# A linear-attention and top-1 expert kernel: weights held by rank of load, three first layers in a row at the change to the experts, and late weight loads from slot 3 on

## The chip, the core and the metric

The kernel runs on one core of a Trainium2 chip, as one program in one launch. What counts is the device time of that launch in microseconds, from inputs in the chip's memory (HBM) to outputs in it. The kernel before takes 1004.49 us (median of three runs, 1004.49 to 1005.99). Its profiled execution spans 1002.1 us.

A core has five engines with instruction streams of their own, which wait for each other by semaphores: TensorE (PE; its weight loads are listed apart as PEld), VectorE (DVE), ScalarE (ACT), GpSimd (POOL) and SyncE (SP). Sixteen DMA engines move data; in this kernel SP and POOL issue the transfers.

## What is computed

Eight batches of eight heads with 576 rows of 64 features go through attention without softmax. The result, 4608 rows of 512, goes through eight experts, and each row through one of them:

```python
def phi(x, c, s):
    r = np.maximum(x, 0.0)
    return np.concatenate([r * c, r * s], axis=-1)   # c, s: cos, sin of the position
kv  = np.einsum('bhsf,bhsd->bhfd', phi(k), v);  z = np.sum(phi(k), axis=2)
x   = einsum(phi(q), kv) / (einsum(phi(q), z) + 1e-6)       # 4608 x 512
logits = x @ w_gate;  e_idx = argmax(logits)                # the expert of a row
gate_w = softmax(logits)[e_idx];  eom = sigmoid(x @ w_output_gate)
for e in range(8):                                          # F = 1024
    h = np.maximum(x[mask] @ w1[e], 0.0);  ye = h @ w2[e]
    out[mask] = gate_w[mask, None] * eom[mask, e, None] * ye
```

The inputs are drawn once and are the same in every run. With them the experts get 305, 493, 580, 0, 986, 569, 398 and 1277 rows, which fill 39 tiles of 128 rows if each expert begins a tile of its own. q, k, v and the weights are fp32; 28.3 MB of q, k and v are read, and 33.6 MB of weights, which become 16.8 MB of fp16 on the way in.

## The kernel before

**Weights.** At the very start GpSimd issues 16 transfers (L121, L122) that bring all weights into two resident tiles, `w1t` and `w2t`, and turn fp32 to fp16 as they do.

**Attention (L136 to L253).** For each batch there are five chunks of 128 rows, the last of 64. SyncE loads `qt`, `kt` and `vt` of a chunk (double buffered, runs of 256 bytes). ScalarE makes `qp` and VectorE `kp`: relu, times cosine into 64 columns and times sine into 64 more. TensorE multiplies `kp` with `vt` for each head (L171), and VectorE adds the product into `kvzg` (L173). TensorE turns `qp` of each head (L178), and ScalarE and VectorE in turn copy the result to `qpt` (L181, L183). When all five chunks of a batch are in, each head's `kvzg` is turned (L187), copied (L189) and multiplied with the gate weights (L191), so that the gates' logits come out of the same product as the rows. Then for each chunk `fx` = `qpt` x `kvzg` (L204); VectorE divides, sums the logits of eight heads (L215), finds the expert and the coefficient, and writes `xch` (L250), which goes to `x_dram`. All of it is fp32, apart from `xch`.

**Routing (L255 to L358).** After the last chunk the counts of the experts are summed over all 40 chunks and every chunk gets the positions of its rows. GpSimd scatters each chunk's row numbers and coefficients to the table `bucket` in HBM (L348). `dst_i`, `pack` and `ni` have one buffer each, so a chunk's scatter must have landed before the next chunk's positions may be written. The table is then read back to `bidx`.

**Experts (L366 to L416).** 42 slots of 128 rows, the largest number that could be needed. A slot's rows are gathered from `x_dram` (L371), turned (L377) and copied (L390), multiplied with 512 x 1024 weights (L395), put through relu (L399), turned (L384), copied (L387), multiplied with 1024 x 512 weights (L406), scaled (L410) and scattered to the output (L411). All is fp16 with fp32 sums. The two layers of neighbouring slots alternate on TensorE.

The order of work on the engines is left to a scheduler that follows the program order and the tiles' dependencies.

Of the kernel before, what the change touches and what calls it, by code (L numbers as in the profile page):

```python
# [10 lines left out]
F32 = mybir.dt.float32  # L12
F16 = mybir.dt.float16
I32 = mybir.dt.int32
ALU = mybir.AluOpType
AF = mybir.ActivationFunctionType
AX = mybir.AxisListType
# [3 lines left out]
def kernel(  # L21
# [21 lines left out]
    E = 8  # L43
    F = 1024
    P = 128
    NCH = 5
    ROWS = [128, 128, 128, 128, 64]
    NG = B * NCH
    NSLOT = 42
    CAP = NSLOT * P  # L50

    constp = ctx.enter_context(tc.tile_pool(name="constp", bufs=1))
    wpool = ctx.enter_context(tc.tile_pool(name="wpool", bufs=1))
    tabs = ctx.enter_context(tc.tile_pool(name="tabs", bufs=1))
    dram = ctx.enter_context(tc.tile_pool(name="drampool", bufs=1, space=bass.MemoryType.DRAM))

    x_dram = dram.tile([N, DM], F16, name="x_dram")
    bucket = dram.tile([CAP, 2], F32, name="bucket")

    ident = constp.tile([P, P], F32, name="ident")  # L60
    make_identity(nc, ident[:])
    ident16 = constp.tile([P, P], F16, name="ident16")
    make_identity(nc, ident16[:])
    u128 = constp.tile([P, P], F32, name="u128")
    make_upper_triangular(nc, u128[:], val=1.0, diag=False)
    ones128 = constp.tile([P, P], F32, name="ones128")
    GP.memset(ones128[:], 1.0)

    s_i = constp.tile([P, NCH], I32, name="s_i")
    GP.iota(s_i[:], pattern=[[128, NCH]], base=0, channel_multiplier=1)  # L70
    th = constp.tile([P, NCH], F32, name="th")
# [3 lines left out]
    th2 = constp.tile([P, NCH], F32, name="th2")  # L75
# [5 lines left out]
    cosc = constp.tile([P, NCH], F32, name="cosc")  # L81
    sinc = constp.tile([P, NCH], F32, name="sinc")

    def поly(dst, coeffs, extra_mul, nm):
        acc = constp.tile([P, NCH], F32, name=nm)
        DVE.memset(acc[:], 0.0)
        for cc in reversed(coeffs):
            DVE.tensor_mul(acc[:], acc[:], th2[:])
            DVE.tensor_scalar_add(acc[:], acc[:], float(cc))
        DVE.tensor_mul(acc[:], acc[:], th2[:])  # L90
        DVE.tensor_scalar_add(acc[:], acc[:], 1.0)
        if extra_mul is not None:
            DVE.tensor_mul(dst[:], acc[:], extra_mul[:])
        else:
            DVE.tensor_copy(dst[:], acc[:])

    поly(sinc, sin_c, th, "acc_s")
    поly(cosc, cos_c, None, "acc_c")

    wg2 = constp.tile([P, H, 16], F32, name="wg2")  # L100
    SP.dma_start(wg2[0:64, :, 0:8], moe_w_gate.rearrange("(h p) e -> p h e", p=64))
    SP.dma_start(wg2[0:64, :, 8:16],
                 moe_w_output_gate.rearrange("(h p) e -> p h e", p=64))

    iota8 = constp.tile([P, E], F32, name="iota8")
    _i8 = constp.tile([P, E], I32, name="_i8")
    GP.iota(_i8[:], pattern=[[1, E]], base=0, channel_multiplier=0)
    DVE.tensor_copy(iota8[:], _i8[:])
    iota_slot = constp.tile([P, 1], F32, name="iota_slot")
    _is = constp.tile([P, 1], I32, name="_is")  # L110
    GP.iota(_is[:], pattern=[[1, 1]], base=0, channel_multiplier=128)
    DVE.tensor_copy(iota_slot[:], _is[:])
    mvals = constp.tile([P, NSLOT], F32, name="mvals")
    _im = constp.tile([P, NSLOT], I32, name="_im")
    GP.iota(_im[:], pattern=[[128, NSLOT]], base=0, channel_multiplier=0)
    DVE.tensor_copy(mvals[:], _im[:])

    w1t = wpool.tile([P, 4, E, F], F16, name="w1t")
    w2t = wpool.tile([P, 8, E, DM], F16, name="w2t")
    for e in range(E):  # L120
        GP.dma_start(w1t[:, :, e, :], moe_w1[e].rearrange("(c p) f -> p c f", p=128))  # L121
        GP.dma_start(w2t[:, :, e, :], moe_w2[e].rearrange("(c p) d2 -> p c d2", p=128))  # L122

    coef_tab = tabs.tile([P, NG], F32, name="coef_tab")
    oh_tab = tabs.tile([P, NG, E], F32, name="oh_tab")
    bidx = tabs.tile([P, NSLOT, 2], F32, name="bidx")
    gidx_i = tabs.tile([P, NSLOT], I32, name="gidx_i")
    sidx_i = tabs.tile([P, NSLOT], I32, name="sidx_i")
    slote_i = tabs.tile([P, 1], I32, name="slote_i")

    with tc.tile_pool(name="attn_b", bufs=2) as ap, \
         tc.tile_pool(name="attn_c", bufs=2) as ap2, \
         tc.tile_pool(name="pskv", bufs=3, space=bass.MemoryType.PSUM) as pskv, \
         tc.tile_pool(name="psgen", bufs=5, space=bass.MemoryType.PSUM) as psgen:

        for b in range(B):  # L136
            qpt = ap.tile([P, H, 576], F32, name=f"qpt{b}", tag="qpt")
            kvzg = ap.tile([P, H, 81], F32, name=f"kvzg{b}", tag="kvzg", bufs=1)
            GP.memset(kvzg[:], 0.0)

            for c in range(NCH):
                rows = ROWS[c]
                s0 = c * 128
                qt = ap2.tile([P, H, D], F32, name=f"qt{b}_{c}", tag="qt")
                kt = ap2.tile([P, H, D], F32, name=f"kt{b}_{c}", tag="kt")
                vt = ap2.tile([P, H, 65], F32, name=f"vt{b}_{c}", tag="vt")
# [300 lines left out]
```

## Time and profile before

| | us | from |
|---|---|---|
| time, median of three | 1004.49 | times |
| span | 1002.1 | profile |
| PE busy | 662.7 (66%), 3257 instructions | profile |
| VectorE busy | 377.0 (38%), 2049 instructions | profile |
| ScalarE busy | 177.9 (18%) | profile |
| GpSimd busy | 152.0 (15%) | profile |
| HBM read, written | 67.45 MB, 15.81 MB | profile |

A share of the span is an average over stages that have different limits. Two parts of the profile help against this. One cuts the span in 40 slices and gives each engine's busy share as a digit. The other, the chain of waits, goes back from the last instruction, at each step to what released it, and so tells which work or which transfer the end waited for at any time. A third table gives the busy time of each engine between two times that the reader picks. The profile's groups of instructions give the mean duration of one. Matmuls are pipelined, so the mean duration of one is longer than the time from one to the next. The pace of a run of them is read from the chain.

### The profile page before, as it was taken

The page shows a single profiled execution, that of the slowest core. Times are in us where ns is not written, and L with a number is a line of the kernel's source. Part 1 is how long each engine was busy: PE and PEld are TensorE (multiplying, and loading weights), DVE is VectorE, ACT ScalarE, POOL GpSimd, SP SyncE. Part 2 cuts the span into 40 slices and gives each one's busy share as a digit, 9 for nine tenths or more (in the row PEclk, how much of TensorE's full clock was granted, in tenths as well). Part 3 has the DMA queues.
Part 4 walks back from the last instruction along what each step waited for, and adds up shares of the span by engine and source line. Part 5 has one row for each costly group of instructions (what it writes and reads, how often), then busy time and mean ns, then how long its engine had stood idle before and what let it go on. Part 6 is the DMA issues. An engine that isn't in the chain of part 4 may idle for free.

```text
span 1002.1 us, 11193 instructions
## 1 busy us (share of the span) xinstructions
PE 662.7 (66%) x3257; PEld 496.6 (50%) x3257; DVE 377.0 (38%) x2049; ACT 177.9 (18%) x509; POOL 152.0 (15%) x245
## 2 busy tenths in 40 slices
PE   0113187997979979799797884223221099999994
PEld 0013176785867858578575683222211045555552
DVE  3101028456283562835528364111111033443342
ACT  1111001314123141231412210000000022222221
POOL 4110000000000000000000001222222134444441
PEclk9999999999999999999999999999999999999998
DMA  9999931412414124141241000000000112222220
GB/s 173 200 200 200 78 79 34 101 42 61 85 50 95 43 61 85 51 95 43 61 84 51 11 17 9 0 0 2 0 0 1 6 63 91 84 83 88 86 85 21
DMA packets 148858, 65.64 MB, mean 65 GB/s; under 512 B 128254, under 2 KB 141054, under 8 KB 148800
## 3 DMA queue, kind: packets, MB, share of 16 engines
q1 hardware_dynamic: 129600, 33.16, 17.5%
q0 software_dynamic: 19200, 31.77, 13.8%
q8 instruction: 29, 0.48, 0.2%
q14 instruction: 29, 0.24, 0.1%
HBM read 67.45 MB, written 15.81 MB: 83 GB/s over the span
## 4 chain that ended last, share of the span: by engine, by line
PE 50%; DMA 26%; DVE 13%; ACT 5%; issue 4%; SPq 1%; POOLq 0%; POOL 0%; ACTq 0%; DVEq 0%
DMA bucket<-pack,dst_i 14%; PE kvp L171 13%; PE fx L204 9%; PE hp L395 7%; DMA qt<-in_q_dram 7%; PE yp L406 7%; PE tp L178 5%; PE kvgp L191 4%; DVE xch L250 4%; DVE glog L215 2%; PE tpk L187 2%; DMA kt<-in_k_dram 2%; PE htsp L384 2%; DMA vt<-in_v_dram 2%; ACT kvt L189 1%
## 5 line engine op out<-in xcount | busy, mean ns | idle before, releaser
L178 PE MATMUL tp<-ident,qp 128*128 128x128 f32 (+1 forms) x320 | 101.2, 423 | 113.9 <-ACT qpt L181 36.9
L171 PE MATMUL kvp<-vt,kp 128*128 128x65 f32 (+1 forms) x640 | 145.6, 412 | 30.5 <-DMA vt<-in_v_dram 28.1
L171 PEld LDWEIGHTS kvp<-vt,kp 128*128 128x128 f32 (+1 forms) x640 | 143.3, 332 | 32.9 <-issue 32.0
L204 PE MATMUL fx<-kvzg,qpt 128*128 128x81 f32 (+1 forms) x640 | 136.1, 406 | 7.4 <-DVE glog L215 7.4
L204 PEld LDWEIGHTS fx<-kvzg,qpt 128*128 128x128 f32 (+1 forms) x640 | 128.9, 310 | 12.2 <-PE fx L204 10.6
L178 PEld LDWEIGHTS tp<-ident,qp 128*128 128x128 f32 (+1 forms) x320 | 55.4, 206 | 158.2 <-ACT qpt L181 74.1
L399 ACT ACTIVATE hs<-hp 128x512 f16<-128x512 f32 x84 | 50.2, 597 | 331.5 <-PE hp L395 331.5
L250 DVE TENSOR_SCALAR xch<-fx,rc 128x64 f16<-128x64 f32 (+1 forms) x320 | 86.8, 273 | 0.0
L395 PE MATMUL hp<-w1t,xts 128*128 x336 | 81.2, 385 | 7.5 <-DVE xts L390 7.5
L406 PE MATMUL yp<-w2t,hts 128*128 x336 | 79.4, 379 | 1.1 <-DVE hts L387 1.1
L173 DVE TENSOR_TENSOR kvzg<-kvzg,kvp 128x260 f32<-128x260 f32 x80 | 32.9, 418 | 110.5 <-PE kvp L171 110.5
L410 DVE TENSOR_SCALAR ysb<-yp,bidx 128x512 f32<-128x512 f32 x42 | 31.5, 751 | 112.8 <-PE yp L406 112.8
L215 DVE SCALAR_TENSOR_TENSOR glog<-fx,rc,glog 128x16 f32<-128x16 f32 (+1 forms) x280 | 62.9, 225 | 0.3
L181 ACT COPY qpt<-tp 128x128 f32<-128x128 f32 (+1 forms) x160 | 39.8, 252 | 119.5 <-PE tp L178 119.5
L183 DVE COPY qpt<-tp 128x128 f32<-128x128 f32 (+1 forms) x160 | 38.6, 266 | 47.8 <-PE tp L178 45.3
L341 DVE CAST dst_i<-dst_f 128x1 int32<-128x1 f32 (+1 forms) x40 | 6.1, 152 | 131.8 <-DMA bucket<-pack,dst_i 131.8
L406 PEld LDWEIGHTS <-hts 128*128 128x128 f16 x336 | 32.8, 98 | 40.6 <-DVE hts L387 1.2
L153 POOL MEMSET vt<- 128x8 f32 x40 | 4.4, 113 | 314.2 <-PE kvp L171 263.2
L395 PEld LDWEIGHTS <-xts 128*128 128x128 f16 x336 | 32.1, 98 | 39.7 <-DVE xts L390 9.1
L411 POOL DMA_INDIRECT out_dram<-ysb,sidx_i x42 | 42.6, 1014 | 56.1 <-DVE ysb L410 37.2
L348 POOL DMA_INDIRECT bucket<-pack,dst_i x40 | 38.6, 966 | 79.3 <-DVE dst_f L338 55.6
L371 POOL DMA_INDIRECT xg<-x_dram,gidx_i x42 | 40.8, 972 | 62.6 <-PE xtsp L377 45.9
(234 smaller groups left out, 661.1 us busy)
## 6 DMA issues: line engine op xcount, KB each, us to landing
qt<-in_q_dram SPq DMA_DIRECT2D x32, 256.0 KB, 3.9
w1t<-in_moe_w_dram POOLq DMA_DIRECT2D x8, 1024.0 KB, 46.4
kt<-in_k_dram SPq DMA_DIRECT2D x32, 256.0 KB, 3.5
vt<-in_v_dram SPq DMA_DIRECT2D x32, 256.0 KB, 3.2
w2t<-in_moe_w_dram POOLq DMA_DIRECT2D x8, 1024.0 KB, 44.0
x_dram<-xch SPq DMA_DIRECT2D x32, 128.0 KB, 1.7
qt<-in_q_dram SPq DMA_DIRECT2D x8, 128.0 KB, 2.8
kt<-in_k_dram SPq DMA_DIRECT2D x8, 128.0 KB, 3.4
```

Of the source, the lines that this page charges most:

```text
L171: PE.matmul(kvp[:, hh, :], kp[0:rows, h, :], vt[0:rows, h, :], start=True, stop=True)
L178: PE.transpose(tp[:, 0:rows], qp[0:rows, h, :], ident[0:rows, 0:rows])
L181: ACT.copy(qpt[:, h, s0:s0 + rows], tp[:, 0:rows])
L191: PE.matmul(kvgp[:, :], kvt_sb[0:64, :], wg2[0:64, h, :], start=True, stop=True)
L204: PE.matmul(fx[h // 4][0:rows, h % 4, :], qpt[:, h, s0:s0 + rows], kvzg[:, h, 0:81], start=True, stop=True)
L215: DVE.scalar_tensor_tensor(glog[0:rows, :], fx[h // 4][0:rows, h % 4, 65:81], rc[0:rows, h:h + 1], glog[0:rows, :], ALU.mult, ALU.add)
L250: DVE.tensor_scalar(xch[0:rows, h * 64:(h + 1) * 64], fx[h // 4][0:rows, h % 4, 0:64], rc[0:rows, h:h + 1], None, ALU.mult)
L371: GP.indirect_dma_start(out=xg[:], out_offset=None, in_=x_dram[:, :], in_offset=bass.IndirectOffsetOnAxis(ap=gidx_i[:, j:j + 1], axis=0))
L395: PE.matmul(hp[:], xts[:, kc, :], w1t[:, kc, bass.ds(ev, 1), fh * 512:(fh + 1) * 512], start=(kc == 0), stop=(kc == 3))
L399: ACT.activation(hs[:, fh * 512:(fh + 1) * 512], hp[:], AF.Relu)
L406: PE.matmul(yp[:], hts[:, fc, :], w2t[:, fc, bass.ds(evp, 1), :], start=(fc == 0), stop=(fc == 7))
L411: GP.indirect_dma_start(out=out[:, :], out_offset=bass.IndirectOffsetOnAxis(ap=sidx_i[:, jj:jj + 1], axis=0), in_=ysb[:], in_offset=None, ...
```

## The change

The kernel is written anew with the same inputs and outputs. It does the following.

- **Own order.** The order of instructions on every engine is written out by hand (`manual_schedule`). Attention is a list of 36 units: 32 of 128 rows, and 4 that put the 64-row tails of two batches together. Every unit names the work on k, the loads and the routing steps that go beside it.
- **Loads.** A partition takes four neighbouring rows, so that runs are 1024 bytes. All q, k and v buffers lie inside the weights' tile `wt` (`own`), whose ranks 2, 3, 4, 6 and 7 are loaded after those buffers are done with.
- **Position factors later.** Only relu is applied to q and k. Cosine and sine go into two copies of v beside each other (`vcs`, 130 columns a head), and once more into the product (`q_mm`: `t` = cosine part, then sine part times sine plus `t`).
- **Half-array products.** The turning of q, q times kv, and k times v are written as pairs of matmuls that use different halves of the array: two heads in rows 0 to 63 and 64 to 127, or outputs in partitions 0 to 63 and 64 to 127. A bank of PSUM collects several heads, and one instruction empties it.
- **Routing along the way.** After nine units `route` finds expert, position and coefficient for all nine chunks with a few wide instructions; its steps are spread over the following units. Rows go straight to their expert's region of `xs`, with row number and coefficient appended, by one indirect scatter for each chunk (`scatter`), with no order among scatters.
- **Weights by rank.** After two of the four groups the experts are ranked by count so far (`ranks`). Weights are loaded in order of rank, from unit 25 on; ranks 4 to 7 from slot 3 on. Each load counts on a semaphore; GpSimd waits for the rank two before, VectorE waits for a slot's rank before it copies `xts`.
- **Early and late slots.** Eight full tiles of the first three groups are slots 0 to 7, so experts start before the last group is routed. 31 more slots follow, and four that are only run if a count says so.
- **The change to the experts.** First layers of slots 0, 1 and 2 stand before the second layer of slot 0. Slots 18 to 36 turn h by a DMA transpose rather than on TensorE.
- Idle matmuls on zeros stand at the start and in the last units, which write to no result.

The core of the diff (the whole kernel function is replaced):

```diff
-    for e in range(E):
-        GP.dma_start(w1t[:, :, e, :], moe_w1[e].rearrange("(c p) f -> p c f", p=128))
-        GP.dma_start(w2t[:, :, e, :], moe_w2[e].rearrange("(c p) d2 -> p c d2", p=128))
...
-            for h in range(H):
-                tp = psgen.tile([P, P], F32, name=f"tp{b}_{c}_{h}", tag="ps")
-                PE.transpose(tp[:, 0:rows], qp[0:rows, h, :], ident[0:rows, 0:rows])
...
-            dst_i = tabs.tile([P, 1], I32, name=f"dst_i_{g}", tag="dst_i")
...
+    def load_w(r, m):
+        if r not in wreg:
+            wreg[r] = GP.value_load(ordi[0:1, r:r + 1], min_val=0, max_val=E - 1)
+            if r > 1:
+                GP.wait_ge(wsem[r % 2], 16 * (r % 2) + 32 * (r // 2))
...
+        def load_half(dst, src, b, hf):
+            SP.dma_start(dst[b % 2][:, 4 * hf:4 * hf + 4, :, :],
+                         src[b, 4 * hf:4 * hf + 4, 0:512, :].rearrange(
+                             "h (p c) d -> p h c d", c=NC4))
...
+        def k_mm(b, c, part=range(4)):
...
+            for s_ in part:
+                for ab in range(2):
+                    PE.matmul(kvp[64 * ab:64 * ab + 64, s_ // 2, o:o + 130],
+                              kr[p0:p1, head(s_, ab), :], vw[p0:p1, head(s_, ab), :],
...
+        def q_tr(i):
...
+            for s_ in range(4):
+                for ab in range(2):
+                    PE.matmul(tp[64 * ab:64 * ab + 64, 128 * s_:128 * s_ + 128],
+                              src[:, head(s_, ab), :], ident[:], start=True, stop=True)
...
+        def q_mm(i, u, x):
...
+                            PE.matmul(qo[t0:t1, 2 * ab + s_, 0:162],
+                                      qT[r0:r0 + 64, s2, t0:t1],
+                                      kvms[...][r0:r0 + 64, 2 * s2:2 * s2 + 2, :],
+                                      start=True, stop=True)
+                d0 = ACT.activation(t, qo[:, :, 0:81], AF.Copy, scale=cosc[:, c:c + 1])
+                d1 = DVE.scalar_tensor_tensor(u[:, h0:h0 + 4, :], qo[:, :, 81:162],
+                                              sinc[:, c:c + 1], t, ALU.mult, ALU.add)
...
+        def h_tr(j):
+            if j in BY_DMA:
+                SP.dma_start_transpose(hts[:], hs[:])
+                return
...
+        wload = {25: [(0, 0)], 26: [(0, 1)], 28: [(1, 0)], 29: [(1, 1)], 31: [(2, 0)],
+                 32: [(2, 1)], 34: [(3, 0)]}
...
+        wload = {3: [(4, 1)], 4: [(4, 0)], 5: [(5, 0)], 6: [(5, 1)], 7: [(6, 0)],
+                 8: [(6, 1)], 9: [(7, 0)], 11: [(7, 1)]}
...
+        q_out(*outs[0])
+        layer1(0, pkv.tile([P, 2, 512], F32, name="hp0", tag="kvp"))
+        x_tr(2)
+        layer1(1)
+        h_tr(0)
...
+        layer1(2)
+        h_tr(1)
+        x_tr(3)
+        step()
+        layer2(0)
...
+        for j in range(3, NMAIN + 1):
...
+            if j < NMAIN:
+                layer1(j)
...
+                    layer2(m)
...
+            for w in wload.get(j, ()):
+                load_w(*w)
```

## The prediction

> **What bounds the kernel now.** I read the busy slices first, because one sum over the span would mix stages with different limits.
>
> ```profile
> PE 0113187997979979799797884223221099999994
> POOL 4110000000000000000000001222222134444441
> DMA  9999931412414124141241000000000112222220
> ```
>
> Each digit is a fortieth of the span, 25 us. There are four stages. At first only DMA is full. From slice 5 TensorE takes over. From slice 24 nothing is busy, GpSimd alone being at 2. From slice 32 TensorE is full again. The table of busy time by stage, cut where those digits change, puts numbers to them (columns: window, length, busy time of PE, PEld, DVE, ACT and POOL, granted clock, DMA share, GB/s):
>
> ```profile
> 0.00:126.00 126.00, 21.32 (x93) 18.50 (x93) 18.26 (x76) 15.00 (x35) 16.83 (x41) 1.00 1.12 169
> 126.00:604.00 478.00, 410.14 (x1779) 342.66 (x1778) 253.49 (x1541) 112.18 (x387) 8.37 (x42) 1.00 0.26 60
> 604.00:793.00 189.00, 52.04 (x211) 39.50 (x211) 34.02 (x305) 0.55 (x3) 43.35 (x78) 1.00 0.01 1
> 793.00:802.00 9.00, 0.00 (x0) 0.00 (x0) 0.41 (x3) 0.00 (x0) 1.94 (x2) 1.00 0.38 19
> 802.00:991.00 189.00, 179.16 (x1176) 95.93 (x1176) 70.24 (x126) 50.16 (x84) 80.51 (x81) 1.00 0.24 80
> 991.00:1002.10 11.10, 0.00 (x0) 0.00 (x0) 0.59 (x1) 0.00 (x0) 0.98 (x1) 0.69 0.00 0
> ```
>
> So 126 us of loading, 478 us of attention at 86% PE, 198 us of routing (189 + 9), 189 us of experts at 95% PE, an 11 us end. What the routing waits for is in the chain of waits, which is in order of time (start, length, what):
>
> ```profile
> 610.83 3.60 DMA bucket<-pack,dst_i
> ...
> 615.47 3.82 DMA bucket<-pack,dst_i
> ...
> 620.31 3.69 DMA bucket<-pack,dst_i
> ```
>
> One of 40 scatters every 4.7 us: the next may not start until the last has landed, since `dst_i` and `pack` have one buffer. The same view gives the price of TensorE work in the expert stage, and the timeline that of fp32 work:
>
> ```profile
> 804.26 3.39 PE hp L395 x8
> ...
> 810.03 1.73 PE yp L406 x8
> 811.75 0.22 PE xtsp L377 x4
> ...
> 816.64 0.45 PE htsp L384 x8
> ```
>
> ```profile
> 279.62 3.64 PE L204 MATMUL fx<-kvzg,qpt 128*128 128x81 f32 x16
> ...
> 287.42 1.31 PE L204 MATMUL fx<-kvzg,qpt 128*64 128x81 f32 x8 [0.68 <-DVE glog L215]
> ```
>
> Eight fp16 matmuls of 512 columns take 1.73 us warm, but 3.39 us just after the idle routing; a transpose takes 0.056. An fp32 matmul appears as two passes (8 heads x 40 chunks are 640 records). With 128 stationary columns a pass takes 0.22 us whether it streams 65 or 81 columns (L171: 16 passes in 3.6 us)[...]. With 64 columns it is (1.31 - 0.35)/7 = 0.14 us, 0.35 being the latency of one.
>
> [...] The trace has the 256 B side: 60 GB/s at 0.26 of the engines is 230 GB/s. [...]
>
> **The change, part by part.** It is a rewrite, so I cost the stages anew rather than subtract.
>
> (a) *Opening.* Weights no longer load at the start; their buffers hold q, k and v. Batch 0 needs 2.1 MB of k and v, 9 us at 230 GB/s, after about 2 us to the first landing; the last half's chain of products, copies and gate matmuls adds about 3 (its tpk, kvt, kvgp, copy round took 1.4 us a head before, here four heads share one). **14 us**, bounds 11 and 20. The constants and the dozen idle matmuls lie under that wait.
>
> (b) *Attention.* 36 units of 128 rows (two 64-row tails share one) in place of 40 chunks. PE in a unit: 16 passes with 64 columns to turn q, 16 with 128 for q times kv, 16 with 64 for k. In series that is 2.2 + 3.5 + 2.2 = 7.9 us; the halves go in pairs to different row or column groups, so perfect pairing gives 3.95. For each batch 4 fp32 transposes at 0.25 (the chain has L178 x8 in 2.00 us) and 16 short passes add 1.0 + 1.1 paired, over 4.5 units 0.45. PE paired: 4.4 us a unit. ACT: three passes over 128x512 for k at 0.6 to 0.72 (L399, L157) and two evacuations of 324 elements, about 0.45 each between the 0.26 of 128 (L181) and the 0.6 of 512 (L399): 2.9. DVE: two of 324 elements at about 0.5 (L173: 0.418 for 260), one of 512 at 0.7 (L410: 0.75), half of a 1.2 us output group (two short ones and two of 256 elements at L173's 0.42), 0.4 of routing: 2.8. [...] DMA: 28.3 MB over 36 units is 0.79 MB, 3.4 us at 230 GB/s[...], plus 0.13 MB of scatter, 0.5. So PE at 4.4 if the weight loads stay in the pace, about 3.2 if pairing hides them and ACT or DMA binds. I take 3.9: **140 us**. Bounds 115 and 36 x 7.9 + 26 = 310.
>
> (c) *Routing.* It goes into the units, a group of nine at a time: some 17 small vector instructions at 0.15 to 0.2 us, the 0.4 above. Scatters carry whole rows, have five index buffers and no order among them, so the 4.7 us rounds vanish; 36 of them take POOL 1 us each beside PE's 3.9 a unit. The last five, the late table (about 25 small vector instructions, 5 us) and the fetch of slot 8 lie under slots 0 to 6, which run on early tiles: 7 slots x 4.1 = 29 us against about 2 + 4 + 9 + 5 + 3 = 23. **0 us on the path**, bound 15.
>
> (d) *Experts.* The drawn tokens make 39 tiles, so the extra slots are skipped. A slot: 16 matmuls 3.46, 4 x-transposes 0.22, 8 h-transposes 0.45: 4.13, against 4.39 before (0.26 waited for xts, now one slot ahead). 19 slots turn h by DMA: 3.68. 20 x 4.13 + 19 x 3.68 = 152.5, and 2.5 for stray waits: **155 us**. The three first layers in a row fill the wait for h and keep the clock up: about 2 us, inside that sum.
>
> (e) *Weights.* Before, 16 loads took about 103 us, so one costs at most 6.2 us of DMA beside the q, k and v loads, 5.2 at the 200 GB/s of slices 1 to 3. Seven start in units 25 to 34, 43 us for 11 x 3.9. One more starts in the first slots and eight from slot 3 to 11. The waits added are GpSimd's on the rank two earlier, with the output scatters queued behind it, and VectorE's ahead of an xts copy. Nine loads with output and fetches, 13.4 MB, need 67 us, while slots 3 to 22, where all must be in, last 78. GpSimd may fall behind 10 to 15 us; five ysb buffers cover 20. **0 us**, bound 40.
>
> (f) *End.* From the last matmul to the end 11 us as before[...], and 2.4 that the time has over the span (1004.5 against 1002.1): **15 us**. The sum is 14 + 140 + 155 + 15 = 324; less 2 for first slots that overlap the last units, **322 us**.
>
> **The rivals.** *Faster still:* pairing hides the weight loads, ACT and DMA bind at 3.2: 322 - 25 = 297. For it, 2.9 and 2.8 us on ACT and DVE; against it, 0.22 a pass. *Weight loads serialize:* pairs share one load path and (b) is 310: 492. [...] *DMA starves the change-over:* 28.3 MB and 4.75 MB of scatters at 230 GB/s and 7 loads at 5.2 are 123 + 21 + 37 = 181 us of DMA work before the first slot, against 154, and late ranks: up to 40 more, 362. *Slower than before:* no pairs, PE cold throughout (twice 310 and 155) and each scatter in turn (36 x 4.7 = 169): 620 + 310 + 169 + 29 = 1128. The 3.39 row shows such a clock[...].
>
> **How the numbers follow.** Forecast 0.52, faster still 0.20, starving 0.12, serial loads 0.15, slower 0.01. The range, 280 to 395, takes in the first three with their bounds and leaves out serial loads and slower, some 0.2 with the tails. Even the serial case is under half the time before: faster 0.985, same 0.005, slower 0.01.
>
> **What would show it.** First expert matmul at 140 to 165 us, with PE full in every slice before; 16 q passes of a unit in under 2.2 us rather than 3.5; no gap between scatters that ends in a scatter's landing; expert slots of 4.1 and 3.7 us; no waits over 1 us on weights. A unit of 7 us, or a stop of PE near slots 18 to 28, would make the forecast wrong.

## The result and the profile after

The kernel takes 341.57 us (median of four, 339.96 to 343.28), against 1004.49 before: a ratio of 0.3403, 95% interval 0.3391 to 0.3416. The forecast was 322 and its range 280 to 395. The way it goes is the forecast's, but the kernel is 20 us slower than forecast, and the experiments ask where they go. In three of the kernels below one execution was some 1 to 2% slower than the rest; the medians move by under 0.2 us without it, and the profile of the run with 256-byte runs is of such an execution.

These are the busy slices of the kernel after, a fortieth of 338.3 us each, that is 8.5 us:

```profile
PE   7899899999999889998768699998999999999980
POOL 7002224338723575576776343441222232232231
PEclk9999999999999999999969699999999999999997
DMA  8999999987998579999998899999937879676911
```

TensorE is at 8 or 9 from the second slice on, with one dent from the twentieth to the twenty-third (161 to 195 us), which is the change to the experts; there the granted clock dips too. DMA, which was at 1 to 4 in the attention before, is mostly at 8 or 9 until about 235 us. The chain of waits is of no use here: it has two pieces, both GpSimd's at the very end. So I cut the span at the stages (window, length, busy time of PE, PEld, DVE, ACT and POOL, granted clock, DMA share, GB/s):

```profile
0.00:20.60 20.60, 16.93 (x155) 9.72 (x155) 11.64 (x61) 6.28 (x16) 6.62 (x38) 1.00 0.99 266
20.60:158.00 137.40, 130.31 (x1941) 109.31 (x1939) 108.96 (x298) 101.21 (x196) 68.01 (x67) 1.00 0.96 240
158.00:180.00 22.00, 16.50 (x95) 8.58 (x96) 15.29 (x46) 4.68 (x7) 15.10 (x17) 0.84 1.15 221
180.00:190.00 10.00, 6.19 (x43) 3.43 (x41) 5.94 (x23) 1.32 (x2) 6.98 (x8) 0.90 0.61 178
190.00:235.00 45.00, 42.94 (x271) 22.57 (x269) 18.91 (x43) 9.78 (x10) 15.07 (x16) 0.95 1.14 234
235.00:330.00 95.00, 93.76 (x537) 46.55 (x535) 33.37 (x77) 25.04 (x25) 24.31 (x25) 1.00 0.73 167
330.00:338.30 8.30, 0.15 (x1) 0.00 (x0) 0.75 (x1) 0.00 (x0) 0.97 (x1) 0.78 0.13 48
```

| step | forecast, us | measured, us |
|---|---|---|
| opening, to the first q product | 14 | 20.6 |
| attention, 36 units | 140 | 137.4 |
| experts, first to last matmul (158.6 to 330.2) | 155 | 171.6 |
| end, with the time over the span | 15 | 8.2 + 3.3 |

Of the 3.3 us over the span, 1.7 belong to the profiled execution (339.96 against 338.3), and 1.6 are what the median execution took longer than the profiled one.

The experts hold most of the difference. A slot in its steady state takes what was forecast: the first layers of slots 14, 15 and 16 start 4.12 us apart, and from slot 21 on, with h turned by DMA, 3.68. In the stages' table TensorE is 93.76 of 95 us busy after 235 us. What is too long lies before: slot 14 starts 73.9 us after slot 0 where 14 x 4.12 = 57.7 would do. Of these **16.2 us**, 5.9 are lost by slot 3, 5.1 more by slot 5, 3.5 by slot 8 and 1.6 by slot 14. Three stops show, and I give them numbers, since the experiments are about them. A smaller loss of 1.3 us stands between slots 6 and 7, which are 5.42 us apart: there TensorE waits for the late table's `valid` (L638). It is the same 5.42 us in the run without late weights.

**Stop 1, slot 2 to 3.** From the timeline (start, length, engine, line, what; in brackets the idle time and what ended it):

```profile
165.11 1.89 PE L764 MATMUL yps<-wt,hts 128*128 x8
...
169.08 1.73 DVE L497 TENSOR_TENSOR oh@3_4_2622<-glog,lmax@3_4_2618 128x40 f32<-128x40 f32 x1
169.68 1.06 POOL L468 TENSOR_TENSOR xr<-wt,rc 128x512 f16<-128x512 f32 x1
171.42 0.74 DVE L771 TENSOR_SCALAR ysb<-yps,xg 128x512 f32<-128x512 f32 x1
...
171.65 0.20 PE L511 MATMUL rk<-oh,u 128*128 128x48 f16 x1 [4.66 <-DVE oh L503]
...
172.22 3.57 PE L764 MATMUL yps<-wt,hts 128*128 x8 [0.25 <-DVE ysb L771]
```

TensorE ends slot 0's second layer at 167.0 and then waits 4.66 us for the last group's one-hot table (L503), because the rank product (L511) is next in its queue. VectorE is 6.37 of 7 us busy there (165 to 172). One of its instructions takes 1.73 us where its neighbours of the same shape take 0.20: it overlaps GpSimd's L468 and ends 0.07 us after it, though by the record it began 0.60 us before it. After the stop TensorE runs at half clock (granted 0.50 from 172.3 to 175.6 us): the second layer of slot 1 takes 3.57 us and not 1.89, and from its start to that of the next second layer 6.79 us pass where 4.12 are ordinary.

**Stop 2, slot 4 to 5.**

```profile
183.72 1.89 PE L764 MATMUL yps<-wt,hts 128*128 x8 [0.43 <-issue]
187.92 1.02 ACT L754 ACTIVATE hs<-hp 128x1024 f16<-128x1024 f32 x1 [7.62 <-remote]
...
189.00 1.03 PE L731 MATMUL htsp<-ident,hs 128*128 128x128 f16 x8 [3.39 <-ACT hs L754]
```

Slot 4's first layer ends at 183.3, but the relu that waits for it starts at 187.92. TensorE's own signal comes 4.6 us late in the record. The second layer of slot 3, whose matmuls end at 185.61 in the record, is signalled at that moment too: VectorE's scaling of it starts at 187.95. Half clock follows again (granted 0.50 from 190.3 to 193.7 us), in slot 5's first layer (3.62 us) and the start of slot 4's second (2.44).

**Stop 3, slot 13 to 14.** SyncE's waits between 158 and 250 us (us in total, times, longest), and what TensorE then waits for:

```profile
SPq L688 <- DMA out_dram<-ysb,xg: 21.6, 4, 6.8
```

```profile
231.64 0.40 PE L698 MATMUL xtsp<-ident,xg 128*128 128x128 f16 x4 [0.81 <-DMA xg<-xs]
```

The fetch of a late slot's rows (L688) needs one of eight `xg` buffers. A buffer comes free when its output scatter, which reads the row numbers in it, has landed, and with the queues at a share of 1.15 (200 to 240 us) the output scatters issued from 189 to 215 us land 8 to 14 us after their issue. So the fetches of slots 12 to 15 are issued 6.0 to 7.2 us apart (205.3, 211.8, 217.8 and 225.0 us), and a slot takes 4.1. Since earlier slots had been slow too, only 1.6 us of it show.

### The profile page after: what moved, and what is told of

It reads as the page before. It is cut to its first block, busy times and chain, and to the rows that moved or that the text cites. A ratio compares the mean times of both kernels' runs of the same rounds, so it can differ in the third digit from the quotient of the medians.

```text
span 338.3 us, 8923 instructions
## 1 busy us (share of the span) xinstructions
PE 306.8 (91%) x3032; PEld 200.2 (59%) x3032; DVE 194.9 (58%) x547; ACT 148.3 (44%) x253; POOL 137.1 (41%) x171
## 5 line engine op out<-in xcount | busy, mean ns | idle before, releaser
L754 ACT ACTIVATE hs<-hp 128x1024 f16<-128x1024 f32 x39 | 39.9, 1024 | 118.3 <-PE hp L746 108.0
L771 DVE TENSOR_SCALAR ysb<-yps,xg 128x512 f32<-128x512 f32 x39 | 29.3, 751 | 84.1 <-PE yps L764 81.8
L764 PE MATMUL yps<-wt,hts 128*128 x312 | 75.9, 387 | 1.9 <-DVE ysb L771 1.5
L746 PE MATMUL hp<-wt,xts 128*128 x312 | 75.8, 387 | 1.6 <-issue 0.8
L468 POOL TENSOR_TENSOR xr<-wt,rc 128x512 f16<-128x512 f32 x36 | 40.8, 1141 | 66.6 <-DVE rc L464 59.7
L445 PE MATMUL qo<-kvm,wt 64*128 64x162 f32 (+1 forms) x640 | 50.6, 309 | 3.1 <-DVE wt L453 2.2
L746 PEld LDWEIGHTS <-xts 128*128 128x128 f16 x312 | 29.6, 100 | 30.9 <-issue 3.2
L445 PEld LDWEIGHTS qo<-kvm,wt 64*128 64x128 f32 (+1 forms) x640 | 40.9, 175 | 10.1 <-DVE wt L453 3.9
L451 ACT ACTIVATE wt<-qo,cosc 128x324 f32<-128x324 f32 x72 | 36.8, 530 | 18.8 <-PE qo L445 16.8
L453 DVE SCALAR_TENSOR_TENSOR wt<-qo,sinc,wt 128x324 f32<-128x324 f32 x72 | 37.1, 550 | 11.9 <-ACT wt L451 7.8
L427 PE MATMUL qtp<-ident,wt 128*64 128x128 f32 x576 | 39.4, 279 | 0.5 <-ACT wt L406 0.5
L427 PEld LDWEIGHTS qtp<-ident,wt 128*64 128x64 f32 x576 | 30.7, 136 | 7.0 <-issue 6.3
L382 PE MATMUL kvp<-wt 128*64 128x130 f32 x448 | 31.1, 277 | 0.8 <-DVE wt L338 0.8
L382 PEld LDWEIGHTS kvp<-wt 128*64 128x64 f32 x448 | 25.3, 137 | 2.1 <-issue 1.0
```

The lines of the kernel that those rows point to most:

```text
L382: PE.matmul(kvp[64 * ab:64 * ab + 64, s_ // 2, o:o + 130], kr[p0:p1, head(s_, ab), :], vw[p0:p1, head(s_, ab), :], start=(c == 0 and s_ % ...
L427: PE.matmul(tp[64 * ab:64 * ab + 64, 128 * s_:128 * s_ + 128], src[:, head(s_, ab), :], ident[:], start=True, stop=True)
L445: PE.matmul(qo[t0:t1, 2 * ab + s_, 0:162], qT[r0:r0 + 64, s2, t0:t1], kvms[b if c < 4 else b - 1 + j][r0:r0 + 64, 2 * s2:2 * s2 + 2, :], s ...
L451: d0 = ACT.activation(t, qo[:, :, 0:81], AF.Copy, scale=cosc[:, c:c + 1])
L453: d1 = DVE.scalar_tensor_tensor(u[:, h0:h0 + 4, :], qo[:, :, 81:162], sinc[:, c:c + 1], t, ALU.mult, ALU.add)
L468: GP.tensor_tensor(xrows[:, slot + x, 0:DM].bitcast(F16).rearrange("p (h d) -> p h d", d=D), u[:, 8 * x:8 * x + 8, 0:64], rc[:, 8 * x:8 * ...
```

## The experiments

All times are medians. Where a table gives slot starts, they are from the profiled run, in us after the first matmul of slot 0.

**The kernel after once more, to see what repeats.**

> The changed kernel once more, to see which of its stops return. If the two stops of PE in slots 0 to 4 (4.7 us before the rank product, 3.4 us before slot 4's turning, each followed by half-clock work) come from the order of the work, both are there again at the same instructions; if the second is an accident of one execution, where PE's signals came 4.6 us late, it is absent here and the time is 3 to 5 us lower. Time 340 to 343.

341.58 us, 0.3378 (0.3366 to 0.3389) of the kernel before. Stops 1 and 2 came at the same instructions; slot 14 started at 233.5 us (232.5 in the first run) though slot 0 was 2.3 us later. So the stops belong to the program. Of the 2.3 us only 1.0 reached slot 14, since stop 3 took 0.3 us here and not 1.6.

**The rank product behind the second layer of slot 1.**

```diff
-        step(3)
         layer2(1)
+        step(3)
```

> One move: the rank product of the last group stands after the second layer of slot 1 instead of before it. Theory (PE's queue waits for VectorE's routing steps, and the cold clock after it costs as much again): the stop of 4.7 us before the rank product shrinks to 1 to 2 us and the half-clock stretch after it goes, so hp of slot 3 starts 5 to 7 us earlier; of that 3 to 7 us arrive at the end. Rival (the late table and the fetch of slot 8 set when slot 8 can start, whatever PE does before): slot 3 earlier, slot 8 at the same time, and a total within 1 us of the changed kernel.

340.50 us, 0.3359 (0.3350 to 0.3368). Slot 3 came no earlier (19.9 after slot 0, before that 18.3). The wait only moved: the second layer of slot 1 now stood idle 5.3 us and was released by VectorE's scaling of slot 0's output (L771, `ysb`). That instruction stands in VectorE's queue behind the routing step. Moving TensorE's instruction alone could not help.

**Batch 0's gates behind its second half.** They stood inside the two opening rounds:

```diff
-            if hf:
-                g_mm(0, 0, 1)
-                idle_mms(ips, 2)
...
-                place_gates()
...
+        place_gates()
+        g_mm(0, 0, 1)
```

> One move: the copies of the gate weights, for which VectorE stood still until 13.1 us, and the product that reads them, go behind batch 0's second half. Theory (the opening is a chain on VectorE that this wait lengthened): unit 0 starts at about 18.6 instead of 20.6 us, total 2 us lower. Rival (the second half of v lands only then, or DMA sets the pace of the first units): unit 0 or the first few units give it back, total within 0.5 us.

341.59 us, 0.3370 (0.3364 to 0.3375). The first unit came 0.07 us earlier, and units 2 and 3 still took 7.5 and 4.7 us (each from its first q product to the next unit's) where others take 3.2. From the timeline of this run:

```profile
12.89 0.36 DVE L356 TENSOR_SCALAR wt<-wt,cosc 128x256 f32<-128x256 f32 x1 [1.87 <-DMA wt<-in_v_dram]
...
18.17 0.82 DVE L298 COPY wpr<-wg 64x64 f32<-64x64 f32 x4
...
20.50 1.60 PE L445 MATMUL qo<-kvm,wt 64*128 64x162 f32 x16
```

VectorE now starts on the second half's v at 12.89 us, when it has landed, and not at 13.76. The copies of the gate weights (L298) give these 0.9 us back, since where they stand now they are in the chain too. So the loads are in at about 13 us, and from there to the first q product lie 7.6 us of scaling, products, copies, turning and gates. The run moved work from one end of this chain to the other; a shorter chain wasn't tried. Stop 2 was shorter in this run and slot 5 came 2.3 us earlier, but slots 6, 12 and 13 took 7.0, 6.4 and 6.2 us, and slot 14 started at 232.6 again.

**Column halves one after the other.**

```diff
-            for s_ in range(4):
-                for ab in range(2):
+            for ab in range(2):
+                for s_ in range(4):
```

> The eight products that turn q are issued four on one half of the columns and then four on the other, instead of alternately. Theory (alternate halves run at the same time): a pass goes from 0.056 to about 0.14 us, as for 64 columns in the kernel before, 16 of them 0.9 to 2.2 us; PE sets the pace of a unit, so 36 x 1.3 = 47 us more. Rival (64 columns are simply cheaper where weight loads run ahead): under 5 us more.

352.72 us, 0.3497 (0.3475 to 0.3518): 11 us more. The 16 passes that turn q in a unit, from the timelines of after and of this kernel:

```profile
58.12 1.09 PE L427 MATMUL qtp<-ident,wt 128*64 128x128 f32 x16
```

```profile
57.46 1.58 PE L427 MATMUL qtp<-ident,wt 128*64 128x128 f32 x16
```

The records of single matmuls tell more. In the kernel after they start in pairs, two 5 to 7 ns apart, and a pair every 109 ns (one record is 279 ns long in the mean, so neighbours overlap). Here a pass without a partner follows its predecessor by 109 ns. So the two passes of a pair, on two column halves, do run at the same time; only where a run of four on one half met the other half did passes still overlap, hence a factor of 1.45 and not 2. That answers the rival of serial weight loads as well: a weight load of this line takes 136 ns by the records (L427, PEld, mean), and the pairs follow each other by 109 ns all the same. Of 0.49 us x 36 = 17.6 us more work for TensorE the time shows 11. Slot 0 came 13.7 us later, so some 4 us were slack ahead of it; about 2 us more came back by slot 14. The theory's 47 us were built on a lone pass of 0.14 us, which this shape doesn't cost.

**Without the late weights.** Now the suspected cause of all that fixes slot 14:

```diff
...
-        wload = {3: [(4, 1)], 4: [(4, 0)], 5: [(5, 0)], 6: [(5, 1)], 7: [(6, 0)],
-                 8: [(6, 1)], 9: [(7, 0)], 11: [(7, 1)]}
+        wload = {}
```

> The eight weight loads of ranks 4 to 7 that stand in slots 3 to 11 are left out; slots of those ranks use rank 3's weights (so the output is another), the waits on weights are capped to ranks 0 to 3, nothing else changes. Theory 'full DMA': the loads keep the sixteen queues full until about 235 us, so output scatters land late, xg buffers come free late, and slot 14's rows come at 232.5 to 233.5 us whatever happens before (three kernels so far). Without the loads the stop before slot 14 goes, only the stop before the rank product in slot 2 stays with its 7 us of half clock; first matmul of slot 14 comes 61 to 66 us after that of slot 0 instead of 73, and the time falls by 8 to 12 us, to 330 to 334. The late signal of hp(4) (4.6 us) should shrink too if it comes from full queues. Rival 'order and routing': the time is lost in the chain of routing, register loads and TensorE's own order in slots 1 to 4, and DMA only fills what is left: slot 14 comes 70 us or more after slot 0 and the time stays at 339 or above.

335.80 us (334.70 to 339.23), 0.3327 (0.3312 to 0.3341): 5.8 us less, and slot 14 came 67.3 us after slot 0, between the two theories. (Rank 5's space holds buffers of the attention as well, `kr2` and `u2`; the description of the change does not name it.) In the stretch after stop 2 TensorE is now full, at a granted clock of 1.00; in the kernel after it had 42.94 us busy, a clock of 0.95 and a DMA share of 1.14 (columns as in the stages' table):

```profile
190.00:235.00 45.00, 44.17 (x304) 24.20 (x303) 20.49 (x47) 11.27 (x11) 10.16 (x11) 1.00 0.32 102
```

From slot 7 on every slot takes exactly 4.12 us. Against the kernel after, 0.9 us are gained by slot 3, 2.8 by slot 5, 5.0 by slot 8 and 6.6 by slot 14. So stop 3 is the smaller part; stop 2 is shorter, with no half clock behind it, and stop 1 stays. Both theories miss their numbers and hold in part: the loads cost some 6 us, and the other 9.6 lie elsewhere. That the loads lengthen stop 2 itself does not follow, since it was as short in the next run, which leaves out only loads that are issued after it (slot 5 at 29.6 us). What was gained there was lost again by slot 14, and here it was not.

**Without the loads of rank 7.** The drawn rows need no such expert:

```diff
...
-                 8: [(6, 1)], 9: [(7, 0)], 11: [(7, 1)]}
+                 8: [(6, 1)]}
```

> Only the two loads of rank 7 (issued in slots 9 and 11) are left out; no slot of these inputs uses that expert, so the output stays. Theory 'full DMA': two loads are about a quarter of the late load volume, but issued late, when slots 12 to 15's rows are on the way; fetches land earlier, slot 14 comes 2 to 5 us earlier and the time falls by 2 to 5 us, to 336.5 to 339.5. Rival 'order and routing', and the other rival that the loads from slot 9 on come behind the fetches that matter: under 1 us.

340.85 us, 0.3365 (0.3359 to 0.3371): less than 1 us, a miss for the theory of full queues as a matter of volume alone. Slot 11 came 2.6 us earlier than in the kernel after, but slots 11 to 13 then took 5.0, 5.2 and 6.0 us, and slot 14 came 73.6 us after slot 0 again. The rival holds: these two loads come behind the fetches that matter.

**Nine more row buffers.**

```diff
-            xg = fsb.tile([P, XW], U16, name=f"xg{j}", tag="xg", bufs=8)
+            if 8 <= j <= 16:
+                if j == 8:
+                    xr4.append(wk.tile([P, GC, XW], U16, name="xr4", tag="xr"))
+                xg = xr4[0][:, j - 8, :]
+            else:
+                xg = fsb.tile([P, XW], U16, name=f"xg{j}", tag="xg", bufs=8)
...
```

> Rows of slots 8 to 16 go to nine buffers of their own (the space of the group's row buffer that is done with), slots 17 on to the eight buffers as before; so no fetch up to slot 16 waits for an output scatter to land. Loads and volume stay the same. Theory 'buffer chain under full DMA': fetches 8 to 16 are issued as soon as the late table is there, the stop before slots 12 to 14 goes, slot 14 comes 3 to 7 us earlier and the time falls by 3 to 6 us, to 336 to 339. Rival 'volume': DMA must move the same bytes by 235 us, and fetches that start earlier push the weight loads back; then a stop moves to a wait on weights or on the output, and the time changes by less than 1.5 us.

340.60 us, 0.3361 (0.3352 to 0.3370). Stop 3 is gone: slots 7 to 15 follow each other by 4.12 us. So the fetch did hang on the landing of scatters. The theory's 3 to 6 us were too many, since this stop is only the 1.6 us between slots 8 and 14; slot 8 came as late as ever.

**Two first layers in a row in place of three.**

```diff
+        layer2(0)
         layer1(2)
         h_tr(1)
         x_tr(3)
         step()
-        layer2(0)
```

> The second layer of slot 0 stands ahead of the first layer of slot 2, so that two first layers stand in a row instead of three. The prediction put the three in a row at about 2 us. Theory 'slot 14 is set by DMA': TensorE waits 1 to 3 us for the turned h of slot 0 and its clock may fall, slots 1 to 3 come that much later, but slot 14 comes within 1 us of where it was and so the time stays within 1 us of 341. Rival: the 2 us and some half clock carry through to the end: 343 to 346.

340.76 us, 0.3356 (0.3348 to 0.3364). Slot 2 came 3.3 us later, slot 3 at the same time as before (18.0 after slot 0), since stop 1 follows anyway. The part of the change that its few words name is worth nothing here.

**A longer instruction stream for TensorE.** In eight runs one of the 16 KB fetches of TensorE's instructions lay beside stop 2 (at 185.8 us in the kernel after).

```diff
-        idle_mms(ips, 12)
+        zf = zt[:, 0:DM].bitcast(F16)
+        for _ in range(76):
+            PE.matmul(ips[:, 0:80], zf[:, 0:P], zf[:, 0:80], start=True, stop=True)
```

> TensorE's instruction stream is made 128 instructions longer at its very start: 76 idle matmuls of 80 columns stand in place of 12 of 512, under the wait for the first loads; nothing else changes. TensorE's instructions are fetched in 16 KB pieces, and in all eight kernels so far one such fetch (at 185 to 188 us) lies beside the stop of TensorE before slot 5, where the signal of slot 4's first layer comes 2 to 4.6 us late. Theory 'instruction supply': the stop goes with the fetch. The fetch moves by about half of the distance of two fetches (8 to 10 us in this stage), the signal of slot 4's first layer is less than 1 us late, slot 5 follows slot 4 by under 5.5 us, and another instruction near the new fetch gets the late signal. Rival 'that place': the late signal stays at slot 4's first layer whatever the fetches do. Both expect the time within 1.5 us of 341, since slot 14's rows are set by the DMA queues.

342.59 us, 0.3386 (0.3376 to 0.3396). The fetches moved to 176.6 and 200.0 us, and none lay near stop 2. The stop stayed:

```profile
188.04 1.02 ACT L754 ACTIVATE hs<-hp 128x1024 f16<-128x1024 f32 x1 [7.84 <-remote]
```

So it isn't this fetch, and my suspicion is out. (Another queue's fetch of 8 KB, at 181.8 us, did not move. In the run with VectorE's order, which follows, fetches lay at 181.7 and 184.1 us and the stop did not come, so neither is enough to make it.)

**VectorE's order, with the nine buffers.**

```diff
...
         x_tr(3)
-        step()
         layer2(0)
+        step()
         scatter(NG - 1, 2)
         scatter(NG - 1, 3)
-        step(3)
         layer2(1)
-        step()
+        step(4)
```

> The nine extra row buffers, and with them the scaling of slot 0's second layer stands ahead of the first routing step on VectorE, and the second layer of slot 1 ahead of the rank product on TensorE. In every kernel so far the second layer of slot 1 waited for that scaling (ysb of slot 0), which stood in VectorE's queue behind the routing step; moving the rank product alone (the run with the second layer of slot 1 ahead of it) left that. Theory 'VectorE's order': the second layer of slot 1 starts within 2.5 us of the end of that of slot 0 (now 5 to 6), the clock stays up, slot 3 comes 13.5 to 16 us after slot 0 instead of 18.3 to 19; with fetches no longer tied to output scatters this carries to slot 14 (67 to 70 us after slot 0) and the time is 336 to 338.5. Rival 'volume': the DMA queues give slot 14 its rows or its weights at 231 us or later whatever comes before, and the time stays at 340 or above.

341.03 us, 0.3369 (0.3361 to 0.3378), the rival's number by the theory's mechanism. Starts after slot 0:

| | slot 3 | slot 5 | slot 8 | slot 14 | slot 18 | time |
|---|---|---|---|---|---|---|
| after | 18.3 | 31.7 | 47.6 | 73.9 | 90.4 | 341.57 |
| without late weights | 17.4 | 28.9 | 42.6 | 67.3 | 83.8 | 335.80 |
| nine more buffers | 19.0 | 32.3 | 47.5 | 72.3 | 88.9 | 340.60 |
| VectorE's order with them | 16.2 | 24.8 | 39.1 | 68.8 | 88.8 | 341.03 |

The second layer of slot 1 started 2.4 us after that of slot 0 had ended (5.7 with the buffers alone), though slowly still (3.32 us for it and not 1.89), and slot 3 came 2.8 us earlier. Stop 2 didn't occur, so slot 8 came 8.4 us earlier. All of it is given back in slots 12 to 16, which take 5.0, 8.1, 4.4, 5.7 and 5.9 us. Who waits there (TensorE's, VectorE's and GpSimd's waits from 205 to 250 us):

```profile
PE yps L772 <- DVE hts L741: 6.1, 4, 2.4
```

```profile
DVE ysb L779 <- DMA out_dram<-ysb,xg: 11.0, 3, 4.7
```

```profile
POOL wt L215 <- ACT hs L762: 10.4, 1, 10.4
POOL wt L215 <- DMA xs<-xr,di@3_0_2539: 8.2, 1, 8.2
```

GpSimd waits 8.2 and then 10.4 us at the first load of ranks 6 and 7, for the rank two before. The releasers that the view names had long been done. The semaphores' own records tell both waits: `wait_ge` in `load_w` (L212) is passed at 207.31 and 222.01 us, each time 0.02 us after the last increment of `wsem` by the second load of rank 4, then of rank 5. The latter was issued at 197.1, so it took 25 us to land. The output scatters stand behind it in GpSimd's queue, the five `ysb` buffers run out, VectorE waits, and the copies of h behind VectorE's wait stop TensorE.

**One late load in every second slot,** on top of that:

```diff
-        wload = {3: [(4, 1)], 4: [(4, 0)], 5: [(5, 0)], 6: [(5, 1)], 7: [(6, 0)],
-                 8: [(6, 1)], 9: [(7, 0)], 11: [(7, 1)]}
+        wload = {3: [(4, 1)], 5: [(4, 0)], 7: [(5, 0)], 9: [(5, 1)], 11: [(6, 0)],
+                 13: [(6, 1)], 15: [(7, 0)], 17: [(7, 1)]}
```

> The run with nine more row buffers and VectorE's new order, and with the eight late loads one in every second slot (3, 5, 7 ... 17) in place of slots 3 to 11. Same bytes, all in by slot 22 as before. In that run slots 13, 15 and 16 took 8.1, 5.7 and 5.9 us since VectorE waited for output scatters to land before it could write ysb, and these stood behind GpSimd's waits of 8.2 and 10.4 us for weights. Theory 'bunched loads': with a load every 8.2 us the queues are just under full, GpSimd finds its ranks landed (waits under 3 us), VectorE waits under 2 us on output scatters, slot 18 comes 83 to 86 us after slot 0 instead of 88.8, and the time is 336 to 338.5. Rival 'volume': the same bytes must pass, so the stops only move to slots 14 to 22, where all weights are waited for, and the time stays at 340 or above.

347.95 us, 0.3483 (0.3467 to 0.3500), slower than the kernel after. Up to slot 18 it went as the theory said: GpSimd's waits for weights were under 2.2 us, slots 7 to 17 took 4.1 to 4.5 us, slot 3 came 15.3 and slot 18 86.2 us after slot 0, although stop 2 was back: from slot 4 to 5 it took 11.0 us. But the last two loads then met the first slots that turn h by DMA:

```profile
247.05 1.89 PE L772 MATMUL yps<-wt,hts 128*128 x8
...
260.49 3.57 PE L772 MATMUL yps<-wt,hts 128*128 x8 [7.66 <-DMA hts<-hs]
```

Between these two lines TensorE did two first layers and then waited 7.66 us for one transposed h. Its transpose was issued at 248.4 us, and of the last two loads, issued at 239.1 and 246.9, the last increment came at 259.2. That the loads held up the transpose is read from these times. The two loads are those of rank 7, which no slot of these inputs needs (see above), and this order without them wasn't tried. As far as these runs go, the place for the loads is bounded from both sides, by the fetches of slots 8 to 16 and by the transposes of slot 18.

**Runs of 256 bytes.** Each load of half a batch is issued for one chunk at a time, rows 128c + p:

```diff
...
-            SP.dma_start(dst[b % 2][:, 4 * hf:4 * hf + 4, :, :],
-                         src[b, 4 * hf:4 * hf + 4, 0:512, :].rearrange(
-                             "h (p c) d -> p h c d", c=NC4))
+            for c in range(NC4):
+                SP.dma_start(dst[b % 2][:, 4 * hf:4 * hf + 4, c, :],
+                             src[b, 4 * hf:4 * hf + 4, 128 * c:128 * c + 128, :].rearrange(
+                                 "h p d -> p h d"))
```

> The loads of q, k and v take rows 128c + p instead of 4p + c for a partition, so that runs in memory are 256 bytes as in the kernel before, not 1024; each load of half a batch is issued as four. Positions and row numbers follow. Theory 'DMA sets the pace from the start to slot 14': [...]some 23 to 27 us more, the opening 2 to 4 us more, and the time is 362 to 369. Rival 'TensorE sets the pace of the attention' (ordinary units are 3.22 us with TensorE full, DMA is only just behind): the loads have slack, the time rises by under 8 us, to 349 at most.

366.89 us, 0.3627 (0.3617 to 0.3636): 25.3 us more, inside the 23 to 27 of the theory, which were my estimate. After, and then this kernel:

```profile
DMA packets 83164, 71.81 MB, mean 212 GB/s; under 512 B 36078, under 2 KB 75566, under 8 KB 83120
```

```profile
DMA packets 159197, 71.83 MB, mean 193 GB/s; under 512 B 136686, under 2 KB 151598, under 8 KB 159152
```

Same bytes, nearly twice the packets. TensorE's work is unchanged, so the queues are as near to the limit of the attention as TensorE is. The four issues for each load are in this number too and weren't tried alone.

## Why the prediction was right, and which steps were off

The cases behind the range hold: under half the time before, no serial weight loads, no scatters in turn. By its steps:

**(a) Opening, 14 us for 20.6: mis-sized in both terms.** I had batch 0's k and v in at 11 us, 9 of them for loading and 2 to the first landing (the loads of `wg` in the kernel before land after 2.3 and 2.4 us). They were in at 12.9 (the run with the gates moved). The queues carry 5.5 MB in the opening (266 GB/s over 20.6 us), since the loads of the next batches run beside them. For the chain from there to the first q product I had 3 us, and it takes about 7.5, the larger part of the error. The bound of 20 for (a) was just missed.

**(b) Attention, 140 us for 137.4: right in sum, by two errors that cancel.** That paired passes run at the same time was my assumption, which nothing in the kernel before shows; the records of single matmuls show it (see the column halves above). The prices were too high. A pair of passes takes 0.109 us with 128 columns streamed (priced 0.14) and 0.137 with 162 (priced 0.22), so an ordinary unit takes 3.22 us. This is near the 3.2 of the "faster still" rival, which was my estimate, but the reason is another: TensorE is what is busy throughout, with ScalarE and VectorE close behind (second line). Units at a batch's border (3.7 to 5.8) and units 2 and 3 bring the mean to 3.82. For the borders I had 0.45 us a unit, for units 2 and 3 nothing. They take 7.3 and 4.7 us, 5.5 more than two ordinary ones, and hold most of batch 1's work on k: 64 passes where two ordinary units have 32. TensorE is busy in them for 10.11 of 11.99 us (first line, columns as in the stages' table), and its waits, 0.8 us for VectorE's L338, 0.7 for ScalarE's L406 and 0.4 for VectorE's L416, name no load:

```profile
26.36:38.35 11.99, 10.11 (x151) 8.47 (x149) 8.09 (x16) 7.98 (x16) 2.47 (x2) 1.00 1.08 291
45.67:48.90 3.23, 3.23 (x51) 2.88 (x49) 3.13 (x8) 3.14 (x7) 2.30 (x2) 1.00 0.87 275
```

That the sum came out right is luck. GpSimd's L468 takes 1.14 us, the mean of 36.

**(c) Routing, 0 us: failed, inside its bound of 15.** Throughput was counted (23 us of work under 29 of slots) and not order. The last group's routing stands in VectorE's queue ahead of `ysb` of slot 0, for which TensorE's second layer of slot 1 waits. With VectorE's order put right slot 3 came 2.8 and 3.7 us earlier in two runs than with the row buffers alone. Part of the stop is the stretched instruction: it took 1.73 us against 0.20 and ended 0.07 us after GpSimd's, though by the record it had started first. What stretches it is not shown. Of 77 VectorE instructions beside L468 in this profile nine took more than one and a half times their usual length. I had counted GpSimd's elementwise work as free beside VectorE.

**(d) Experts, 4.13 and 3.68 us a slot: exact** (4.12 and 3.68), and the three first layers in a row are worth nothing, where I had put 2 us inside the sum.

**(e) Late weights, 0 us: failed, inside its bound of 40.** The volume was near: 67 us were estimated for nine loads with fetches and outputs, and the queues are full from slot 0 to 235 us, some 76 (shares of 1.15 and 1.14), but for the dip at stop 2 (0.61). The last weights land at 244.5 us and slot 22, which waits for all, starts at about 262. VectorE's waits that end in a weight load are 1.3 us at the longest, and only at slot 0 does TensorE then wait, for 0.75 us. What I left out is latency in a full queue: a scatter lands after 8 to 14 us (those issued from 189 to 215) and a weight load after up to 20 (25 in the run with VectorE's order), and buffers, eight `xg` and five `ysb`, are held as long. I had taken that the five cover 20 us. In the kernel after the `xg` buffers end first, and with these mended the `ysb` buffers. The run without the loads gives the price, 5.8 us, of which this chain of buffers (stop 3) is 1.6; how the loads cost the rest is not shown.

**(f) End, 15 us for 11.5:** the last output lands sooner than before, 8.2 us after the last matmul and not 11. (The 11.5 hold the 1.6 us by which the median execution exceeds the profiled one. Of the 15, the 11 and 2.4 were read from the kernel before; the rest was my estimate.)

Of the 20 us, then, +6.6 are the opening, -2.6 attention, +16.6 the experts, -3.5 the end, and 2.6 the overlap that I took off and that didn't come (2.0) with the gap before slot 0 (0.6). Of the experts' 16.6, 5.8 are shown to be the late weights. That most of the rest is stops 1 and 2 is read from the slots, and no run shows it as time saved: with the late loads in place, what was gained before slot 8 was taken back behind it. The mended order without late loads wasn't tried.

Of the signs that I had named, the first expert matmul at 158.6 us, the 16 q passes in 1.09 us and the slots of 4.12 and 3.68 us came as forecast. One sign against the forecast came too, a unit of 7 us: unit 2, with 7.3. And VectorE waited over 1 us for weights twice, 1.3 at the longest. Neither was large enough to undo the sum. The rival of starved queues at the change stayed away, since they moved 266 and 240 GB/s in the opening and the attention, where it was worked out with 230; slot 0 starts at 158.6 us.

**Open:** why stop 2 happens. Of the thirteen profiles of the kernel after and its variants twelve have it, always at slot 4's first layer, with a signal 1.9 to 6.8 us late. It isn't the instruction fetch that was moved, it needs no late weight loads (2.1 us of idle stay without them), and of two programs that differ only in loads issued after it one didn't have it and the other had it at its longest. In the kernel after it lies beside GpSimd's last five row scatters and what follows them, where the DMA share falls to 0.61. But the run without the stop has these scatters there too (179.3 to 186.3 us) and a share of 0.66 from 180 to 190 us, so neither alone makes it.

None of the kernels tried beats the kernel after by more than its times scatter, apart from the one that leaves loads out and needs them.

## What to carry to other kernels

When transfers fill the queues, count buffers by latency and not by volume: a buffer whose release is a landing is held 8 to 14 us here, and its scatter can stand behind a wait for a weight load before that (8.2 and 10.4 us in the run with VectorE's order), and whatever waits in order behind such a wait is part of the price. When a stop is found, look for who is queued behind whom on every engine it touches before moving one instruction; then ask what the gained time will run into, since a stage that waits for transfers gave it back here. A place for background loads has two ends; a shift that clears one stop can make another at the next stage.

## What the runs showed that I had not expected

- Two fp32 passes on two column halves start 5 to 7 ns apart, and a pair comes every 109 ns; a lone pass takes the same 109. So pairing is worth a factor of two here.
- A VectorE instruction of 0.17 to 0.20 us took 1.7 to 1.8 us beside GpSimd's 512-element instruction, twice in the last group's routing; most VectorE instructions beside it were not stretched (68 of 77 in the kernel after).
- TensorE's signal to another engine came up to 6.8 us after the matmuls that it stands for (the run with a load in every second slot), at one place of the program and with no cause that the profile names.
- After stops of 4.66 and 3.39 us TensorE ran 3.57 and 3.62 us for what otherwise takes 1.89, at a granted clock of 0.50; with what follows, each of the two stops costs 2.7 to 2.8 us on top of itself (6.79 and 6.94 us for a round of 4.12). Granted clock over 172 to 180 us: 0.64. A stop of 2.4 us was followed by 3.32 us (VectorE's order), one of 2.1 us by none of this (without late weights).
